# Pairs of tiles: softmax and z transfers in another place, sums of w_in in halves, a12 first in the closing pair

## The chip, the cores and the metric

One NeuronCore of a Trainium2 chip runs the program. The metric is the device time of one execution in microseconds; three runs of the kernel before gave 482.71, 483.19 and 483.50, and 483.19 is their median. Engines are named as in the profile: PE (TensorE), DVE (VectorE), ACT (ScalarE), POOL (GpSimd), SP (SyncE).

## The reference

Attention within chunks of 64 tokens (8 batches, 8 heads, 576 tokens, 64 wide), then a feed-forward layer with a SoLU and a layer norm on the 4608 x 512 result, all in float32:

```python
scores = scale * np.matmul(q_c, k_c.transpose(0, 1, 2, 4, 3))   # chunks of 64
attn = softmax(scores)                                          # with + 1e-09 in the sum
x = np.matmul(attn, v_c) -> (4608, 512)
h = x @ w_in                                                    # 512 -> 1024
solu = h * softmax(h)
ln = (solu - mean) / sqrt(var + 1e-06) * g_ln
return ln @ w_out                                               # 1024 -> 512
```

## The kernel before

**Tiles.** The 4608 tokens are 36 tiles of 128. Products in float32 are made of three fast ones: each operand is split into a rounded high part and a low rest (`x_top` and `x_bottom`, `z_top` and `z_bottom`, `wi_h` and `wi_l`), and high times low, high times high and low times high are summed in PSUM.

**Stages.** Tiles 0 to 4 run in an order written out by hand. Tiles 5 to 9 run singly in a loop (line 1212): `ffn_in` (24 matmuls), attention of two later tiles after each odd tile, and three thirds (`third`, 8 matmuls each) of the product with `w_out` of an earlier tile. Tiles 10 to 35 run in 13 pairs (`pair`, line 1108). A pair makes its h by Strassen's scheme, seven products of 6 matmuls each (`strassen`: a11, s2, s1, s3, then s4, a12, a22), in two PSUM banks pa and pb that alternate; between s3 and s4 and after the attention stand 24 matmuls each on `w_out` (`product`; PSUM tile po). The attention (`scores` and `values`, PSUM tiles sx and sy) of the tiles of the next pairs follows a22.

**Prepared sums.** Strassen's scheme wants sums of blocks of `w_in` (`t_sum`, `t_top`, `t_bottom` for t3 and t2; `t_quarter` for t1). POOL makes them while tiles 5 to 8 run: t3 in tile 5, t2 and two quarters of t1 in tile 6, the other two quarters in tile 8. The quarters go through a scratch tile of the name t_f. The tile `signs` (the identity and its negative, needed by `t_product` in the first pair) has the same tag t_f with one buffer, so it takes the scratch's place in memory.

**What sets the order.** From tile 5 on every engine works its instructions off in the order of the code. A wait of one instruction holds all that stand behind it on its engine. In a pair, `softmax_e` (ACT), `softmax_b` (a sum and a reciprocal on DVE, then a multiplication on POOL) and `attn_turn` (a transposition of 32 x 32 blocks on DVE into a_b, then 8 transfers of 64 KB into attn_t, 4 from SP and 4 from ACT or POOL) prepare the probabilities for the next `values`. `pair_moves` issues 16 transfers of 64 KB from z_b to z_t that bring the finished z of the pair before into its transposed place: 8 from SP at once, 8 from POOL through `issue`. `h_sum` is the DVE addition that empties pb, `act.copy(h0[:, left], a)` the copy on ACT that empties pa. The matmuls of s4, a12 and a22 carry the waits for all transfers that the attention reads (`waits`), one each. All recorded operations have the line of the recording helper, 50, in the profile.

Of the kernel before, what the change touches and what calls it, by code (L numbers as in the profile page):

```python
# [8 lines left out]
F32 = mybir.dt.float32  # L9
# [49 lines left out]
def chunk_attention_then_solu_ffn(  # L59
# [351 lines left out]
    def softmax_e(i):  # L411
        e = st[i, "e"]
        act.activation(e, e, AF.Exp, scale=SCALE)
# [387 lines left out]
    def whole(parts):  # L801
        for _ in parts:
            pass
# [56 lines left out]
    TW = {}  # L860
# [7 lines left out]
    def f32(w):  # L868
        return [x.bitcast(F32) for x in w]

    def t_sum(of, less, more=()):

        f = raw_t[0]
        if of is not None:
            pool.tensor_tensor(out=f, in0=f32(of)[0], in1=f32(of)[1], op=ALU.add)
        for x in f32(less):
            pool.tensor_tensor(out=f, in0=f, in1=x, op=ALU.subtract)
        for x in f32(more):
            pool.tensor_tensor(out=f, in0=f, in1=x, op=ALU.add)

    def t_room():
        def room(dt):
# [9 lines left out]
        return rest  # L892

    def t_top(name):
        pool.tensor_copy(out=TW[name][0], in_=raw_t[0])

    def t_bottom(name):
        high, low = TW[name]
        pool.tensor_tensor(out=low, in0=raw_t[0], in1=high.bitcast(F32), op=ALU.subtract)

    signs = []

# [45 lines left out]
    def x_top(i, n):  # L948
        f, (high, low) = XO[i][n]
        act.copy(high, f)  # L950

    def x_bottom(i, n):
        f, (high, low) = XO[i][n]
        pool.tensor_tensor(out=low, in0=f, in1=high.bitcast(F32), op=ALU.subtract)
# [25 lines left out]
    def h_sum(to, of, bank_):  # L980
        dve.tensor_tensor(out=to, in0=of, in1=bank_, op=ALU.add)
# [47 lines left out]
    def z_top(i, f=slice(0, NFC)):  # L1029
        zt, zh, _ = z_views(i)  # L1030
        act.copy(zh[:, f], zt[:, f])

    def z_bottom(i, f=slice(0, NFC)):
        zt, zh, zl = z_views(i)
        dve.tensor_tensor(
            out=zl[:, f], in0=zt[:, f], in1=zh[:, f].bitcast(F32), op=ALU.subtract
        )
# [65 lines left out]
    def issue(todo, n):  # L1103
        for f, args in todo[:n]:
            f(*args)
        del todo[:n]

    def pair(i):
        opening, closing = i == first_pair, i + 2 >= NT
        if not banks:  # L1110
            whole_h.close()
            ps_b = ctx.enter_context(tc.tile_pool(name="ps_b", bufs=1, space=PSUM))
            banks.extend(ps_b.tile([P, HALF], F32, name=n) for n in ("pa", "pb"))
        a, b = banks
        h0, h1 = (work.tile([P, FF], F32, name="z") for _ in range(2))
        HZ[i], HZ[i + 1] = h0, h1
        out1 = queue[0][0]
        softs = pending[:]
        pending.clear()
        zmoves = pair_moves(i - 2)  # L1120

        z_top(out1)
        strassen(i, "a11", a, B11)
        act.copy(h0[:, left], a)
        z_bottom(out1)
        for m in softs[:1]:
            softmax_e(m)
        strassen(i, "s2", b, TW["t2"])
        h_sum(h0[:, right], h0[:, left], b)
        x_top(i, "s3")  # L1130
        x_bottom(i, "s3")
        for m in softs[1:]:
            softmax_e(m)
        strassen(i, "s1", a, TW["t1"])
        issue(zmoves, 2)
        for m in softs:
            whole(softmax_b(m))
        evict()
        strassen(i, "s3", b, TW["t3"])
        if opening:  # L1140
            t_product("t4", B21, TW["t2"], 0)
        if not opening:
            spread(i - 1)
        for n in ("s4", "a12", "a22"):
            x_top(i, n)
        h_sum(h1[:, left], h0[:, right], b)
        x_bottom(i, "s4")
        for m in softs:
            attn_turn(m)
        issue(zmoves, 12)  # L1150
        least1 = h_out((h1[:, left], h1[:, right]), a, None)
        dve.tensor_tensor(out=h0[:, right], in0=h0[:, right], in1=a, op=ALU.add)
        for p in range(1 if closing else 3):
            product()
            if opening and p == 1:
                t_product("t4", B21, TW["t2"], 1)
        for n in ("a12", "a22"):
            x_bottom(i, n)
        if not opening:
            power(i - 2)  # L1160
            power(i - 1)
        for m in (i + 4, i + 5):
            if m < NT:
                turn(m)
        load_some(9)
        store_rest()

        out0 = queue[0][0]
        waits = (soon.pop(i + 2, []) + soon.pop(i + 3, []))[::-1]
        strassen(i, "s4", a, B22, waits, 6 * NCH2)  # L1170
        if not closing:
            kept.append(out1)
            evict()
            z_top(out0)
        least0 = h_out((h0[:, right], h0[:, right]), a, None)
        strassen(i, "a12", b, B21, waits, 3 * NCH2)
        least0 = h_out((h0[:, left], h0[:, left]), b, least0)
        strassen(i, "a22", a, TW["t4"], waits)
        pair_exp(i, 0, least0)
        least1 = h_out((h1[:, left], h1[:, left]), a, least1)  # L1180
        pair_exp(i, 1, least1)
        if closing:
            return
        z_bottom(out0)
        attention(i)
        for m in (i + 4, i + 5):
            if m < NT:
                load_v(m)
        x_pair(i + 2)
        x_sums(i + 2)  # L1190
        pair_mul(i)
        pair_mul(i + 1)
        for _ in range(3):
            product()
        kept.append(out0)
        pair_mean(i)
        spread(i)
        x_halves(i + 2)
        if i + 4 < NT:
            softmax_a(i + 4)  # L1200
            pending.append(i + 4)
        pair_mean(i + 1)
        pair_turn(i)
        if i + 5 < NT:
            softmax_a(i + 5)
            pending.append(i + 5)
        pair_turn(i + 1)
        load_some(9)
        store_rest()

    first_pair = PAIRS
    for i in range(first, first_pair):
        order.on = i >= ORD
        odd = i % 2 == 1
        turning = i + 1 == first_pair
        if i == first:
            z_turn(i - 1)
            load_batch(next_batch)
            next_batch += 1
        load_v(i + 3)  # L1220
        z_split(queue[0][0], slice(0, NFC))
        if not odd:
            softmax_e(i + 3)
            whole(softmax_b(i + 3))
            attn_turn(i + 3)
            x_high(i + 1)
            if i == first_pair - 4:
                t_sum(None, (), B11)
                t_top("t2")
                t_bottom("t2")  # L1230
                rest_of_room()
            if i == first_pair - 2:
                for x in range(2, 4):
                    t_quarter("t1", B12, B11, x)
        load_some(LOADS[i][0])
        whole(ffn_in(i))
        if odd:
            for m in (i + 1, i + 2):
                scores(m + 2)
                values(m)  # L1240
        if turning:
            load_v(i + 4)
        whole(solu_a(i))
        third()
        if i == first_pair - 5:
            rest_of_room = t_room()
            t_sum(B22, B12)
            t_top("t3")
            t_bottom("t3")
        if odd:  # L1250
            softmax_a(i + 3)
            softmax_e(i + 3)
            if turning:
                x_pair(i + 1)
                x_sums(i + 1)
            else:
                x_high(i + 1)
        else:
            x_low(i + 1)
        whole(solu_b(i))  # L1260
        if odd:
            if turning:
                x_halves(i + 1)
            else:
                x_low(i + 1)
            whole(softmax_b(i + 3))
            attn_turn(i + 3)
        else:
            for m in (i + 4, i + 5):
                turn(m)  # L1270
        third()
        variance(i)
        if i == first_pair - 4:
            for x in range(2):
                t_quarter("t1", B12, B11, x)
        third()
        load_some(LOADS[i][1])
        if turning:
            pair_turn(i)
            signs.append(work.tile([P, 2, P], F32R, name="signs", tag="t_f", bufs=1))  # L1280
            act.copy(signs[0][:, 0], ident)
            act.activation(signs[0][:, 1], ident, AF.Copy, scale=-1.0)
        else:
            z_turn(i)
        store_rest()
        if odd:
            softmax_a(i + 4)
            if turning:
                pending.append(i + 4)
# [55 lines left out]
```

## Time and profile before

| what | us |
|---|---|
| median of 3 runs | 483.19 |
| the profiled execution | 485.89 |
| its span, first to last instruction | 484.1 |
| PE busy | 462.5 (96%) |
| DVE busy | 373.4 (77%) |
| POOL busy | 312.8 (65%) |
| ACT busy | 287.2 (59%) |

PE is busy 96% of the span with 4123 matmuls, and the granted clock is 1.0 but for the first slices of the span (mean 0.995), which is the level of 2.4 GHz. A busy PE is what the records model, so a short wait may hide in it: it is better seen in the start times of matmuls that follow each other. The other engines matter where a matmul waits for them.

### The profile page before, as it was taken

Reading aid. Unit: us, or ns where it says so; the run is one execution under the profiler, and the core shown is the slowest. Engines: PE = TensorE matmul, PEld = TensorE weight load, DVE = VectorE, ACT = ScalarE, POOL = GpSimd, SP = SyncE. Lnnn points to the kernel's source line nnn. Section 1 sums busy time; section 2 is a strip of 40 time slices with the busy share of each in tenths; the row PEclk is TensorE's granted clock in tenths of the full one; section 3 lists DMA queues with packets and bytes.
Section 4 is the critical chain, followed back from the end, with each engine's and each line's share of the span. In section 5 each row is a group of like instructions: output and inputs, shape, how many; then the busy total and the mean of one; then the engine's idle time right before and its main releaser. Section 6 shows DMA issues by size and latency. Waiting matters only on the chain.

```text
span 484.1 us, 11452 instructions
## 1 busy us (share of the span) xinstructions
PE 462.5 (96%) x4123; PEld 361.8 (75%) x4123; DVE 373.4 (77%) x582; ACT 287.2 (59%) x511; POOL 312.8 (65%) x452
## 2 busy tenths in 40 slices
PE   6799999999998999999999989999999999999997
PEld 5655888777876777767777767787777777777776
DVE  2899987799876796969797969796979797955530
ACT  2675885446455393839393928383939393838451
POOL 0339458899986376766676766767667675758340
PEclk9899999999999999999999999999999999999999
DMA  9999888857795767776717866677681717141231
GB/s 231 297 235 320 140 142 175 178 143 157 150 188 123 153 134 161 161 157 140 199 27 163 156 157 149 155 166 169 148 197 32 193 35 184 43 135 49 61 108 43
DMA packets 193767, 72.06 MB, mean 149 GB/s; under 512 B 177128, under 2 KB 177648, under 8 KB 193328
## 3 DMA queue, kind: packets, MB, share of 16 engines
q1 hardware_dynamic: 186528, 58.63, 54.1%
q0 software_dynamic: 4736, 9.45, 8.0%
q10 hardware_dynamic: 2448, 3.28, 2.6%
q8 instruction: 32, 0.52, 0.5%
q14 instruction: 23, 0.19, 0.1%
HBM read 36.70 MB, written 9.44 MB: 95 GB/s over the span
## 4 chain that ended last, share of the span: by engine, by line
PE 56%; DMA 17%; SPq 9%; DVE 7%; ACT 5%; issue 3%; POOL 3%; ACTq 0%; DVEq 0%; POOLq 0%
PE po L50 26%; PE pa L50 10%; DMA attn_t<-a_b 10%; SPq L50 9%; PE ph L50 9%; DMA z_t<-z_b 5%; PE pb L50 5%; PE sx L50 4%; PE sy L50 3%; DMA nat_z<-in_q_dram 2%; ACT z_h L50 2%; DVE a_b L50 1%; ACT z L50 1%; DVE z_b L50 1%; DVE z L50 1%
## 5 line engine op out<-in xcount | busy, mean ns | idle before, releaser
L50 PE MATMUL po<-wo_l,z_h 128*128 128x512 f32 x280 | 111.2, 397 | 0.4 <-ACT z_h L50 0.4
L50 PE MATMUL po<-wo_h,z_l 128*128 128x512 f32 x280 | 109.7, 392 | 1.2 <-DVE z_l L50 1.2
L50 PE MATMUL po<-wo_h,z_h 128*128 128x512 f32 x280 | 109.5, 391 | 0.0
L50 POOL DMA_DIRECT2D z_t<-z_b x136 | 68.6, 510 | 10.9 <-DVE z_b L50 9.0
L50 POOL TENSOR_TENSOR x_s<-x_p 128x256 f32<-128x256 f32 x26 | 23.4, 899 | 68.2 <-ACT x_p L50 67.2
L50 POOL TENSOR_TENSOR x_t<-x_p,x_t 128x256 fp32r<-128x256 f32 x65 | 48.5, 757 | 24.8 <-ACT x_t L50 22.7
L50 PEld LDWEIGHTS po<-wo_h,z_l 128*128 128x128 f32 x280 | 52.6, 188 | 14.0 <-DVE z_l L50 3.0
L50 ACT ACTIVATE o_sb<-po,r 128x512 f32<-128x512 f32 (+1 forms) x36 | 24.4, 676 | 64.5 <-DMA attn_t<-a_b 46.3
L50 PEld LDWEIGHTS po<-wo_l,z_h 128*128 128x128 f32 x280 | 52.6, 188 | 12.3 <-ACT z_h L50 0.9
L50 PEld LDWEIGHTS po<-wo_h,z_h 128*128 128x128 f32 x280 | 52.6, 188 | 10.5
L50 DVE TENSOR_TENSOR z_l<-z_t,z_h 128x1024 fp32r<-128x1024 f32 (+1 forms) x36 | 43.6, 1210 | 12.8 <-ACT z_h L50 8.9
L50 ACT CAST z_h<-z_t 128x1024 fp32r<-128x1024 f32 (+1 forms) x36 | 34.9, 969 | 30.7 <-DMA attn_t<-a_b 17.1
L50 PE MATMUL pa<-wi_h,x_t 128*128 128x512 f32 x156 | 49.3, 396 | 2.2 <-DMA attn_t<-a_b 1.3
L50 DVE STREAM_TRANSPOSE z_b<-z 128x1024 f32<-128x1024 f32 x33 | 40.8, 1236 | 11.0 <-ACT z L50 5.8
L50 ACT ACTIVATE z<-z,z_sum 128x1024 f32<-128x1024 f32 x34 | 39.1, 1150 | 3.4 <-DVE z L50 3.2
L50 PE MATMUL pb<-t_w,x_t 128*128 128x512 f32 x156 | 40.8, 397 | 0.1
L50 POOL TENSOR_TENSOR e<-e,s_rinv 128x512 f32<-128x512 f32 x31 | 32.3, 1059 | 10.8 <-DVE s_rinv L50 10.4
L50 ACT ACTIVATE sq<-z 128x1024 bf16<-128x1024 f32 x36 | 37.6, 1046 | 2.5 <-POOL z L50 2.5
L50 PEld LDWEIGHTS pa<-wi_h,x_t 128*128 128x128 f32 x156 | 29.2, 188 | 11.2 <-DMA attn_t<-a_b 4.2
L50 ACT ACTIVATE z_b<-z,h_nmax 128x1024 f32<-128x1024 f32 x26 | 29.9, 1148 | 12.7 <-DVE h_nmax L50 12.2
L50 DVE SCALAR_TENSOR_TENSOR z<-z,z_b 128x1024 f32<-128x1024 f32 x26 | 36.2, 1426 | 0.0
L50 PEld LDWEIGHTS pb<-t_w,x_t 128*128 128x128 f32 x156 | 28.3, 188 | 10.4 <-ACT e L50 4.5
(140 smaller groups left out, 995.9 us busy)
## 6 DMA issues: line engine op xcount, KB each, us to landing
out_dram<-o_sb SPq DMA_DIRECT2D x35, 256.0 KB, 3.6
z_t<-z_b SPq DMA_DIRECT2D x128, 64.0 KB, 2.0
z_t<-z_b POOLq DMA_DIRECT2D x128, 64.0 KB, 2.6
q_st<-in_q_dram SPq DMA_DIRECT2D x96, 72.0 KB, 3.1
k_st<-in_k_dram SPq DMA_DIRECT2D x96, 72.0 KB, 2.9
v_sb<-in_v_dram SPq DMA_DIRECT2D x27, 256.0 KB, 5.0
w_raw<-in_moe_w_out_dram SPq DMA_DIRECT2D x4, 1024.0 KB, 9.3
attn_t<-a_b SPq DMA_DIRECT2D x60, 64.0 KB, 3.6
```

The source lines that it names most:

```text
L50: ins = make(*args, **kwargs)
```

## The change

Six edits, none of which changes what is computed:

- `t_sum`, `t_top` and `t_bottom` work on each of two halves of 512 columns in place of 1024 at once.
- In `pair`, the exponentials of the two softmax tiles move ahead (the first into the pair before, ahead of `x_halves`), then come the copy of a11's product, `x_top` of s3, `z_top`; `softmax_b` goes ahead of `h_sum`, `z_bottom` behind it.
- All 8 z transfers of POOL are issued together, behind the two multiplications of the softmax and ahead of the low part of s4.
- `attn_turn` moves ahead of the second `h_sum`.
- In the closing pair (tiles 34 and 35) the product a12 stands ahead of s4.
- `signs` is written at the end of tile 8 in place of the end of tile 9.

```diff
--- before.py
+++ after.py
@@ -870,13 +870,14 @@
 
     def t_sum(of, less, more=()):
 
-        f = raw_t[0]
-        if of is not None:
-            pool.tensor_tensor(out=f, in0=f32(of)[0], in1=f32(of)[1], op=ALU.add)
-        for x in f32(less):
-            pool.tensor_tensor(out=f, in0=f, in1=x, op=ALU.subtract)
-        for x in f32(more):
-            pool.tensor_tensor(out=f, in0=f, in1=x, op=ALU.add)
+        for m in range(NCH2):
+            f = raw_t[0][:, m]
+            if of is not None:
+                pool.tensor_tensor(out=f, in0=f32(of)[0][:, m], in1=f32(of)[1][:, m], op=ALU.add)
+            for x in f32(less):
+                pool.tensor_tensor(out=f, in0=f, in1=x[:, m], op=ALU.subtract)
+            for x in f32(more):
+                pool.tensor_tensor(out=f, in0=f, in1=x[:, m], op=ALU.add)
 
     def t_room():
         def room(dt):
@@ -892,11 +893,15 @@
         return rest
 
     def t_top(name):
-        pool.tensor_copy(out=TW[name][0], in_=raw_t[0])
+        for m in range(NCH2):
+            pool.tensor_copy(out=TW[name][0][:, m], in_=raw_t[0][:, m])
 
     def t_bottom(name):
         high, low = TW[name]
-        pool.tensor_tensor(out=low, in0=raw_t[0], in1=high.bitcast(F32), op=ALU.subtract)
+        for m in range(NCH2):
+            pool.tensor_tensor(
+                out=low[:, m], in0=raw_t[0][:, m], in1=high[:, m].bitcast(F32), op=ALU.subtract
+            )
 
     signs = []
 
@@ -1119,22 +1124,20 @@
         pending.clear()
         zmoves = pair_moves(i - 2)
 
-        z_top(out1)
+        for m in softs[-1:]:
+            softmax_e(m)
         strassen(i, "a11", a, B11)
         act.copy(h0[:, left], a)
-        z_bottom(out1)
-        for m in softs[:1]:
-            softmax_e(m)
+        x_top(i, "s3")
+        z_top(out1)
+        x_bottom(i, "s3")
+        for m in softs:
+            whole(softmax_b(m))
         strassen(i, "s2", b, TW["t2"])
         h_sum(h0[:, right], h0[:, left], b)
-        x_top(i, "s3")
-        x_bottom(i, "s3")
-        for m in softs[1:]:
-            softmax_e(m)
+        z_bottom(out1)
+        issue(zmoves, 8)
         strassen(i, "s1", a, TW["t1"])
-        issue(zmoves, 2)
-        for m in softs:
-            whole(softmax_b(m))
         evict()
         strassen(i, "s3", b, TW["t3"])
         if opening:
@@ -1143,11 +1146,10 @@
             spread(i - 1)
         for n in ("s4", "a12", "a22"):
             x_top(i, n)
+        for m in softs:
+            attn_turn(m)
         h_sum(h1[:, left], h0[:, right], b)
         x_bottom(i, "s4")
-        for m in softs:
-            attn_turn(m)
-        issue(zmoves, 12)
         least1 = h_out((h1[:, left], h1[:, right]), a, None)
         dve.tensor_tensor(out=h0[:, right], in0=h0[:, right], in1=a, op=ALU.add)
         for p in range(1 if closing else 3):
@@ -1167,14 +1169,18 @@
 
         out0 = queue[0][0]
         waits = (soon.pop(i + 2, []) + soon.pop(i + 3, []))[::-1]
+        if closing:
+            strassen(i, "a12", b, B21)
+            least0 = h_out((h0[:, left], h0[:, left]), b, None)
         strassen(i, "s4", a, B22, waits, 6 * NCH2)
         if not closing:
             kept.append(out1)
             evict()
             z_top(out0)
-        least0 = h_out((h0[:, right], h0[:, right]), a, None)
-        strassen(i, "a12", b, B21, waits, 3 * NCH2)
-        least0 = h_out((h0[:, left], h0[:, left]), b, least0)
+        least0 = h_out((h0[:, right], h0[:, right]), a, least0 if closing else None)
+        if not closing:
+            strassen(i, "a12", b, B21, waits, 3 * NCH2)
+            least0 = h_out((h0[:, left], h0[:, left]), b, least0)
         strassen(i, "a22", a, TW["t4"], waits)
         pair_exp(i, 0, least0)
         least1 = h_out((h1[:, left], h1[:, left]), a, least1)
@@ -1195,10 +1201,11 @@
         kept.append(out0)
         pair_mean(i)
         spread(i)
-        x_halves(i + 2)
         if i + 4 < NT:
             softmax_a(i + 4)
+            softmax_e(i + 4)
             pending.append(i + 4)
+        x_halves(i + 2)
         pair_mean(i + 1)
         pair_turn(i)
         if i + 5 < NT:
@@ -1277,12 +1284,13 @@
         load_some(LOADS[i][1])
         if turning:
             pair_turn(i)
+        else:
+            z_turn(i)
+        store_rest()
+        if i == first_pair - 2:
             signs.append(work.tile([P, 2, P], F32R, name="signs", tag="t_f", bufs=1))
             act.copy(signs[0][:, 0], ident)
             act.activation(signs[0][:, 1], ident, AF.Copy, scale=-1.0)
-        else:
-            z_turn(i)
-        store_rest()
         if odd:
             softmax_a(i + 4)
             if turning:
```

ACT at the end of tile 8 and of tile 9, around `signs` (x_t, x_p: operands of the first pair; o_sb: a finished output; z_h: high part of z; z, h_sum<-ph,h_nmax: the exponential of tile 9's h). Before, at the end of tile 9:

```order
L50 ACTIVATE sq,ssq<-z 128x1024
L50 ACTIVATE o_sb<-po,r 128x512
L50 CAST signs<-ident 128x128
L50 ACTIVATE signs<-ident 128x128
L50 CAST z_h<-z_t 128x1024
L50 COPY z<-pa 128x512
L50 ACTIVATE e_103<-e_103 128x4x128
```

Now, at the end of tile 8:

```order
L50 ACTIVATE sq,ssq<-z 128x1024
L50 ACTIVATE o_sb<-po,r 128x512
L50 CAST signs<-ident 128x128
L50 ACTIVATE signs<-ident 128x128
L50 CAST z_h<-z_t 128x1024
L50 ACTIVATE z,h_sum<-ph,h_nmax 128x1024
L50 ACTIVATE e_102<-e_102 128x4x128
```

The two writes of `signs` now stand ahead of tile 9's z_h and of all that ACT does for tile 9. In the built program the first of them waits for POOL, for the last subtraction of the last quarter of t1, which reads the scratch t_f; before, it had no wait.

DVE at the start of a pair (z_b: transposition of the last z of the pair before; s_sum, s_rinv: `softmax_b`; z<-z,pb: `h_sum`; z_l: `z_bottom`; a_b: `attn_turn`). Before:

```order
L50 STREAM_TRANSPOSE z_b<-z 128x8x4x32
L50 TENSOR_TENSOR z_l<-z_t,z_h 128x1024
L50 TENSOR_TENSOR z<-z,pb 128x512
L50 TENSOR_REDUCE s_sum<-e_102 128x8
L50 RECIPROCAL s_rinv<-s_sum 128x8
L50 TENSOR_REDUCE s_sum<-e_103 128x8
L50 RECIPROCAL s_rinv<-s_sum 128x8
L50 TENSOR_TENSOR z<-z,pb 128x512
L50 STREAM_TRANSPOSE a_b<-e_102 128x8x2x32
L50 STREAM_TRANSPOSE a_b<-e_103 128x8x2x32
```

Now:

```order
L50 STREAM_TRANSPOSE z_b<-z 128x8x4x32
L50 TENSOR_REDUCE s_sum<-e_102 128x8
L50 RECIPROCAL s_rinv<-s_sum 128x8
L50 TENSOR_REDUCE s_sum<-e_103 128x8
L50 RECIPROCAL s_rinv<-s_sum 128x8
L50 TENSOR_TENSOR z<-z,pb 128x512
L50 TENSOR_TENSOR z_l<-z_t,z_h 128x1024
L50 STREAM_TRANSPOSE a_b<-e_102 128x8x2x32
L50 STREAM_TRANSPOSE a_b<-e_103 128x8x2x32
L50 TENSOR_TENSOR z<-z,pb 128x512
```

Four instructions of the softmax stand ahead of the first addition out of pb, where z_l stood, and the transpositions a_b are ahead of the second.

POOL in a pair, from the softmax's multiplications (e) to the low parts of the last two products' operands (x_t). Before:

```order
L50 DMA z_t<-z_b 32x512 x2
L50 TENSOR_TENSOR e_102<-e_102,s_rinv 128x4x128
L50 TENSOR_TENSOR e_103<-e_103,s_rinv 128x4x128
L50 TENSOR_TENSOR x_t<-x_s,x_t 128x256
L50 DMA z_t<-z_b 32x512 x6
L50 TENSOR_TENSOR x_t<-x_p,x_t 128x256 x2
```

Now:

```order
L50 TENSOR_TENSOR e_102<-e_102,s_rinv 128x4x128
L50 TENSOR_TENSOR e_103<-e_103,s_rinv 128x4x128
L50 DMA z_t<-z_b 32x512 x8
L50 TENSOR_TENSOR x_t<-x_s,x_t 128x256
L50 TENSOR_TENSOR x_t<-x_p,x_t 128x256 x2
```

The multiplications no longer wait behind two transfers, the other six transfers are ahead of the low part of s4, and the closing pair has the same order without the multiplications.

## Rows read from the trace of the kernel before

**Rows 1.** Waits of PE, 160 to 440 us: in total, times, longest.

```profile
PE pa L50 <- DMA attn_t<-a_b: 2.6, 6, 0.7
```

**Rows 2.** Windows from attention to attention: length, busy by engine, PEclk, DMA share, GB/s.

```profile
408.85:431.94 23.09, 23.09 (x219) 18.57 (x218) 17.71 (x29) 13.74 (x27) 16.35 (x25) 1.00 0.41 112
sum 264.35, PE 259.91 PEld 203.40 DVE 218.27 ACT 165.11 POOL 181.07; mean PE 23.63 PEld 18.49 DVE 19.84 ACT 15.01 POOL 16.46
```

**Rows 3.** Timeline of PE in one pair: start, length, operation, tiles, [idle before].

```profile
346.85 1.52 PE L50 MATMUL pb<-t_w,x_t 128*128 128x512 f32 x6
...
349.86 1.62 PE L50 MATMUL pb<-t_w,x_t 128*128 128x512 f32 x6
```

**Rows 4.** Waits of PE from 425 us to the end, as in rows 1.

```profile
PE po L50 <- DVE z_l L50: 0.5, 1, 0.5
PE pa L50 <- DVE z L50: 0.4, 1, 0.4
PE pa L50 <- ACT z L50: 0.4, 1, 0.4
PE po L50 <- ACT z_h L50: 0.4, 2, 0.2
```

**Rows 5.** Groups of POOL by form, 84 to 142: busy, mean ns, idle before.

```profile
L50 POOL TENSOR_TENSOR t_w<-t_w,wi_l 128x1024 f32<-128x1024 f32 x2 | 4.8, 2419 | 0.2
```

**Rows 6.** Timeline of DVE at 88 us.

```profile
88.69 3.34 DVE L50 TENSOR_TENSOR z_l<-z_t,z_h 128x1024 fp32r<-128x1024 f32 x1 [0.86 <-ACT z_h L50]
```

**Rows 7.** Timeline of POOL, last quarter of t1, 136 to 142 us.

```profile
138.05 1.60 POOL L50 TENSOR_TENSOR t_f<-t_f,wi_h 128x256 f32<-128x256 f32 x1
...
141.01 0.73 POOL L50 TENSOR_TENSOR t_w<-t_f,t_w 128x256 fp32r<-128x256 f32 x1
```

**Rows 8.** Timeline of ACT, end of tile 8 and of tile 9.

```profile
136.19 1.05 ACT L50 CAST z_h<-z_t 128x1024 fp32r<-128x1024 f32 x1 [0.62 <-DMA attn_t<-a_b]
...
150.07 0.29 ACT L50 CAST signs<-ident 128x128 fp32r<-128x128 f32 x1
...
151.41 0.58 ACT L50 COPY z<-pa 128x512 f32<-128x512 f32 x1
151.89 0.63 ACT L50 ACTIVATE e<-e 128x512 f32<-128x512 f32 x1
```

**Rows 9.** Timeline of DVE in tile 9.

```profile
140.32 1.23 DVE L50 TENSOR_REDUCE h_nmax<-ph 128x1 f32<-128x1024 f32 x1 [1.26 <-PE ph L50]
```

**Rows 10.** Timeline of PE in the first pair.

```profile
152.04 1.67 PE L50 MATMUL pa<-t_w,x_t 128*128 128x512 f32 x6 [1.31 <-ACT z L50]
...
164.21 0.70 PE L50 MATMUL pa<-wi_h,x_t 128*128 128x512 f32 x2 [0.91 <-DVE kT L50]
```

**Rows 11.** Timeline of DVE at the start of a pair.

```profile
347.93 1.18 DVE L50 TENSOR_TENSOR z_l<-z_t,z_h 128x1024 fp32r<-128x1024 f32 x1
349.03 0.68 DVE L50 TENSOR_TENSOR z<-z,pb 128x512 f32<-128x512 f32 x1
349.63 0.68 DVE L50 TENSOR_REDUCE s_sum<-e 128x8 f32<-128x520 f32 x1
...
350.47 0.64 DVE L50 TENSOR_REDUCE s_sum<-e 128x8 f32<-128x520 f32 x1
...
352.19 1.48 DVE L50 STREAM_TRANSPOSE a_b<-e 128x512 f32<-128x512 f32 x2
```

**Rows 12.** Timeline of ACT at the same place.

```profile
344.96 0.41 ACT L50 CAST x_t<-x_p 128x256 fp32r<-128x256 f32 x1 [1.05 <-POOL x_p L50]
```

**Rows 13.** Timeline of POOL in the same pair.

```profile
350.87 2.06 POOL L50 TENSOR_TENSOR e<-e,s_rinv 128x512 f32<-128x512 f32 x2
...
353.56 2.97 POOL L50 DMA_DIRECT2D z_t<-z_b  x6
```

**Rows 14.** Windows of the same pair, as in rows 2.

```profile
353.00:355.00 2.00, 2.00 (x11) 1.65 (x10) 2.00 (x5) 0.00 (x0) 2.00 (x4) 1.00 0.40 98
355.00:360.00 5.00, 5.00 (x22) 3.70 (x20) 3.38 (x9) 0.69 (x1) 4.39 (x10) 1.00 0.92 227
```

## The prediction

> **What bounds the kernel now.** I read the windows first, then the waits of PE, then timelines of the places that the diff touches. In the window behind the last attention of the pairs PE is busy for all of its 23.09 us at a granted clock of 1.00, and the eleven windows before and with it, one for each attention of the pairs, sum to 264.35, of which PE is busy 259.91 [rows 2]. So PE sets the time: an edit gains only what it takes from the waits of PE, and it loses what it adds to them. In the pairs most of these waits are for the attention's transfers: 2.6 us in six waits of the bank pa [rows 1], and some more of pb. A busy row of matmuls can hide a little waiting: eleven windows of 23.09 would be 253.99, so up to 10.4 us of the eleven depend on neighbours. Much of that is work of POOL, DVE and ACT that some pairs must wait for; only the waits for attn_t, with the refill behind each (5 us by my reading, half of it in rows 1), are touched by the diff. The rest of PE's waits stands at the end: four of 0.4 to 0.5 us behind 425 us [rows 4].
>
> The sum is made on the profiled execution, 485.89 us, whose span is 484.1. It is 0.6% above the median 483.19; I apply the differences to the median, as the waits are of the same length in both by a first estimate.
>
> **Sums of w_in in halves, with `signs` ahead.** POOL's two-input operations take 2.419 us on 1024 columns [rows 5] and 0.73 on 256 [rows 7]; the line through both gives 1.30 on 512, so an operation split in two costs 2 x 1.30 - 2.42 = 0.18, and 0.26 with one more start of 0.08 between (the gap between POOL's rows in tile 8). Five operations of t3 and four of t2 are split: 9 x 0.26 = 2.3 us on POOL. The bound below zero: the softmax's multiplications, also 512 wide with two inputs, step by about 1.05 (two in 2.06) [rows 13], by which a split would save 0.24, or 9 times about 1.5 to 2 us. I take 1.30, as the sums read operands of the form that the line was made from.
>
> Who waits for POOL there? In before nobody on PE, as the quarters of t1 end at 141.01 + 0.73 = 141.74 [rows 7] and t1 is first read later. Now the first write of `signs` waits for that last subtraction, and it stands in ACT's queue ahead of tile 9's z_h, which in before ran from 136.19 for 1.05 [rows 8]. One thing comes back: POOL's row at 138.05 took 1.60 where its like takes 0.73 [rows 7], as DVE's two-input z_l ran beside it; z_l now comes after it, so 0.85 is saved. The last quarter ends at 141.74 + 2.3 - 0.85 = 143.2 (139.4 to 144). Behind it come the two writes (about 0.46 in all with the wait's end), z_h 1.05, z_l 1.1, and only then DVE's h_nmax of tile 9: 143.2 + 2.64 = 145.85, where it started at 140.32 [rows 9]: 5.5 us later. Tile 9's exponential, its x_p copies and the chain over POOL to the first operands of the first pair stand in line behind that. They have no slack to swallow it: at the first pair PE already waited 1.31 for ACT's copy of pa [rows 10], which started at 151.41 [rows 8]. Back come 0.82, as between 150.07 and that copy stood two writes and z_h (1.34) and now one exponential (its row is 0.63, about 0.5 of it to the next start) [rows 8], and 0.67 of the 0.91 that PE waited for the attention's k at 164.21 [rows 10], since a_b moves up by one h_sum in the first pair too. 5.5 - 0.8 - 0.7 = **+4.1**, from +0.2 (POOL 1.5 sooner, 139.4) to +4.8.
>
> In tile 5, where t3 is made, z_l took 3.34 [rows 6], blocked by POOL's 1024-column row; with halves about 1 us of that goes. But the transfers that POOL issues behind the sums go out later by about 1.7 and PE meets them at the next attention: 0, from -0.9 to +1.5.
>
> What the row of 3.34 shows is that a z_l beside a two-input operation of POOL waits for the end of it. The Trainium skill says the same ("SBUF — State Buffer", section "Who interferes with whom"): DVE and GpSimd share a port pair as an exclusive lock, a DVE operation with two SBUF inputs contends with GpSimd's reads, and the second blocks wholly. It speaks for halves (a shorter lock) and against the next part, where z_l is put right behind POOL's multiplications: by it a_b gains the 0.3 of the next part, without it 1.0, and the pairs' sum would be nearer to its lower end of -4.0.
>
> **The pair, eleven windows.** Before, DVE does z_l (347.93) and then h_sum (349.03) [rows 11]; s2 ends at 346.85 + 1.52 = 348.37, and s3, which needs the bank that h_sum empties, starts at 349.86 [rows 3], 0.15 after h_sum's end. So s3 already hangs on h_sum. Now two pairs of sum and reciprocal stand in z_l's place. From one to the next is 350.47 - 349.63 = 0.84 [rows 11], so h_sum starts at 347.93 + 1.68 = 349.61, **0.58 later** than before, in each pair. That is a new wait of PE; s1 cannot cover it, as it has run by then. The exponential that moves into the pair before costs nothing: ACT waited 1.05 for x_p where it will stand [rows 12], against 0.63 for the exponential [rows 8]; were that cover gone, x_t would come 0.63 later.
>
> For this the waits for attn_t go. `attn_turn` moves ahead of the second h_sum, POOL's multiplications no longer stand behind two transfers and s1's stretch, and POOL's z transfers, six of which issue from 353.56 [rows 13], are out by then. In before the 16 DMA engines stand at a share of 0.40 from 353 to 355 and at 0.92 from 355 to 360 [rows 14]: the z transfers move out of the full stretch into the empty one, and the attention's have it to themselves. The a_b themselves, at 352.19 [rows 11], come only about 0.3 earlier, as z_l now stands ahead of them and is blocked by POOL's multiplications (without the block it would be 1.0). A window then is 23.09 + 0.58 = 23.67, and eleven are 260.4; I add 0.7 for waits that stay: 261.1 - 264.35 = **-3.3**, from -1.4 (all 2.6 of rows 1 stay) to -4.0 (none stays).
>
> **Behind the last attention.** PE waits at 433 and 434 for z_h (0.2) and z_l (0.5) [rows 4], with 0.27 of refill at each; the last z transfers of POOL land before the attention's, so both go: **-1.25** (-1.3 to 0).
>
> **The closing pair.** With a12 ahead of s4 the waits for ACT's z (0.4), DVE's z (0.4) and one z_h (0.2) [rows 4], with refill 1.6 in all, go, since between a product and the reader of its bank lies another product. But a12's low operand is made by POOL, behind all eight z transfers (six take 2.97, so eight about 4.0 [rows 13]) and the low part of s4, which a12 did not have to wait for: I put this new wait at 0.95. Sum **-0.65**, from -1.6 to +0.3.
>
> **Rivals.**
> - *The pairs gain more or POOL loses less.* If halves go as the multiplications do (1.05), the quarters end at 139.4 and the start costs 0.2 rather than 4.1: 478.2; if only part of this holds, about 480. For it: the multiplications are the nearest rows in width. Against: they are fed by a broadcast reciprocal, another form of operand.
> - *The transfers land no sooner.* If the engines are the limit and not the place of issue, 2.6 us of waits stay and the pairs give -1.4: 484.0. For it: share 0.92 [rows 14]; against it: 0.40 just before. The Trainium skill's rule ("DMA: Bandwidth & Descriptors", section "Issuing engines are not separate DMA queues") is that all transfers run on the same 16 engines whoever starts them; the stretch of 0.92 agrees, the dip before it does not bear on it.
> - *Slower: the wait of `signs` at its full size.* If POOL gets no 0.85 back, the last quarter ends at 144, the start costs 4.8, and if the waits for attn_t stay in part (-1.6) and the closing pair's new wait eats its gain (0), the sum is +4.8 - 1.6 - 1.25 = +2.0: 485.1. It decides as soon as the start costs more than the 5.2 that the other three parts give.
>
> **How the numbers follow.** 483.19 + 4.1 - 3.3 - 1.25 - 0.65 = **482.1** (chance 0.40). About 480: 0.22. 484.0: 0.20. 485.1: 0.18. Range 479.5 to 484.9: below, half of the first term's span (2.6 less); above, just under the slower rival. About 0.2%, 1.0 us, is what a measurement of this kernel can tell: faster than 482.2, slower than 484.2. The forecast lies at that edge, so a little over half of it and all of the 480 case count as faster (0.46), the rest of it and most of the 484.0 case as the same (0.29), the slower rival and a part of the 484.0 case as slower (0.25).
>
> **What the profile after would show.** Right: sums of 512 columns at 1.30 on POOL; ACT idle from about 136 to 143 ahead of the cast to signs, and h_nmax of tile 9 near 146, with waits of PE of about 4 us between 142 and 165; s3 of each pair waiting for DVE's h_sum, 0.58 later than now; no waits for attn_t; windows near 23.67; none for z_h and z_l at the last attention; in the closing pair one wait of a12 for POOL's x_t. Wrong: windows above 24 with waits for attn_t, sums near 1.05, or an ACT that passes `signs` with no idle time.

## The result: slower, and the profile after

The changed kernel takes 487.93 us (median of 4) where the kernel before took 483.05 beside it: a ratio of 1.0104 (95% interval 1.0082 to 1.0127), 4.9 us slower. The forecast was 482.1, and the range ended at 484.9. The profiled execution after spans 486.5 us.

The shown execution of before (span 484.1) is one of its slower ones, so before was profiled once more (the run b_again below, span 482.5), and that trace is the better measure. Here both are cut at the starts of the attentions. The rows give length, busy time of PE, PEld, DVE, ACT and POOL with instructions, the granted clock, DMA share and GB/s. First before, in its second profile:

```profile
89.23:115.22 25.99, 24.79 (x226) 19.89 (x225) 24.45 (x29) 12.54 (x21) 25.24 (x24) 1.00 0.78 159
115.22:140.98 25.76, 24.78 (x225) 19.75 (x224) 20.80 (x31) 12.64 (x20) 24.09 (x35) 1.00 0.85 172
140.98:168.34 27.36, 25.17 (x227) 19.97 (x226) 19.03 (x31) 13.71 (x27) 16.43 (x27) 1.00 0.64 134
168.34:430.81 262.47, 258.56 (x2400) 204.09 (x2399) 218.25 (x363) 165.25 (x308) 180.90 (x275) 1.00 0.64 142
430.81:482.50 51.69, 46.62 (x283) 37.48 (x282) 22.13 (x35) 27.73 (x50) 19.85 (x36) 1.00 0.20 62
```

And the same stretches after:

```profile
89.18:119.04 29.86, 26.68 (x225) 20.74 (x224) 22.89 (x29) 12.64 (x21) 28.53 (x32) 0.94 0.86 159
119.04:143.06 24.02, 24.02 (x226) 19.91 (x225) 19.23 (x29) 11.48 (x19) 21.68 (x35) 1.00 0.76 161
143.06:174.11 31.05, 26.11 (x228) 19.80 (x227) 21.01 (x32) 14.79 (x28) 16.98 (x28) 1.00 0.57 118
174.11:434.13 260.02, 252.42 (x2400) 205.00 (x2399) 224.47 (x363) 168.97 (x309) 181.30 (x275) 1.00 0.62 143
434.13:486.50 52.37, 46.37 (x283) 37.56 (x282) 22.76 (x35) 26.74 (x49) 20.42 (x35) 1.00 0.19 61
```

Row by row: +3.9 in tiles 5 to 7, where t3 is made; -1.7 in tiles 7 to 9; +3.7 from there through the first pair, where `signs` waits; -2.5 in the eleven windows of the pairs; +0.7 behind the last attention. The waits of PE after, in total, times and longest, over the whole span, name the places:

```profile
PE pb L50 <- DVE z L50: 7.6, 11, 0.9
PE ph L50 <- DMA attn_t<-a_b: 2.9, 2, 2.6
PE po L50 <- ACT z_h L50: 2.2, 2, 2.0
...
PE pa L50 <- DVE h_nmax L50: 0.9, 1, 0.9
...
PE pb L50 <- POOL x_t L50: 0.6, 1, 0.6
```

The first line is s3 waiting for h_sum in eleven pairs; it stands where [rows 1] had the attention's transfers, which no longer appear for pa. The second is tile 7, the third `signs` (2.0 of it), the last two are the closing pair.

The split between the first two rows depends on the execution: in the runs with the sums whole (pool_late aside) the first stretch takes 26.0 to 27.5 us and the second 24.5 to 25.9. Their sum, 50.8 to 51.8 there but for one run (pairs_closing, 53.3), is 53.9 after, so that 2 to 3 us stay of the +3.9, and 2.2 against b_again.

### The profile page after: what moved, and what is told of

Same layout as the page of the kernel before. It is cut to its first block, busy times and chain, and to the rows that moved or that the text cites. A ratio compares the mean times of both kernels' runs of the same rounds, so it can differ in the third digit from the quotient of the medians.

```text
span 486.5 us, 11435 instructions
## 1 busy us (share of the span) xinstructions
PE 456.0 (94%) x4123; PEld 364.3 (75%) x4123; DVE 379.0 (78%) x582; ACT 289.9 (60%) x511; POOL 315.1 (65%) x461
## 3 DMA queue, kind: packets, MB, share of 16 engines
q10 hardware_dynamic: 2448, 3.28, 2.3%
## 4 chain that ended last, share of the span: by engine, by line
PE 48%; DVE 17%; POOL 13%; ACT 8%; DMA 6%; issue 4%; SPq 2%; DVEq 0%; ACTq 0%; POOLq 0%
PE po L50 21%; PE pa L50 8%; PE pb L50 7%; PE ph L50 6%; POOL x_p L50 5%; PE sx L50 3%; DVE z_b L50 3%; DVE s_sum L50 3%; ACT z L50 3%; DVE z L50 3%; PE sy L50 3%; POOL x_t L50 2%; DMA nat_z<-in_q_dram 2%; POOL x_s L50 2%; SPq L50 2%
## 5 line engine op out<-in xcount | busy, mean ns | idle before, releaser
L50 ACT ACTIVATE o_sb<-po,r 128x512 f32<-128x512 f32 (+1 forms) x36 | 24.5, 681 | 68.9 <-DMA attn_t<-a_b 43.6
L50 DVE TENSOR_TENSOR z_l<-z_t,z_h 128x1024 fp32r<-128x1024 f32 (+1 forms) x36 | 50.9, 1413 | 16.8 <-ACT z_h L50 12.2
```

The source lines that it names most:

```text
L50: ins = make(*args, **kwargs)
```

## The experiments

All times are medians, the ratios are to the kernel before on the same chip. The medians of that kernel beside the runs lie between 483.05 and 484.27, so a difference between times of different groups of runs is good to about 1 us; where it matters, the traces are compared stretch by stretch.

**b_again**: before, unchanged.

> The kernel before, unchanged, profiled once more. The shown profile of before lasted 485.89 us where the timed runs have a median of 483.05, so 2.8 us of waits in it may be of that execution alone. Theory 'its waits for attn_t vary': the new profile is near 483 and PE waits for attn_t between 160 and 440 us are under 2 us, where they were 3.6 (2.6 of pa and 1.0 of pb). Rival 'profiling adds it everywhere': about 486 again with the same waits.

483.92 us, ratio 0.9998 (0.9979 to 1.0018); single runs lie between 481.9 and 485.6. The profiled span was 482.5, and the eleven windows sum to 262.47, where [rows 2] had 264.35. So the theory holds in its direction: 1.9 us of the windows in [rows 2] were of that execution. The waits did not vanish, though: 3.1 us for attn_t in ten places, where under 2 was expected.

**pairs_alone**: before with the edits inside the pairs alone (the hunks on `softmax_e`, `softmax_b`, `z_bottom`, `issue`, `attn_turn`).

> Before with the edits inside the pairs only (exponentials, softmax_b, z_bottom, z transfers, attn_turn), without the halves, without signs ahead, without a12 first. Theory 'each edit has its own place': the trace of after gains 4.4 us on before from 165 to 433 us, so 478.7; if the waits for attn_t of the shown profile were partly of that execution (see b_again), the gain is 4.4 - 2.4 = 2 and the time 481. Rival 'the pairs are where the loss is' (the new wait of s3, 0.62 in eleven pairs, is not paid back in timed runs): 483.05 + 2 or more, 485.

478.85 us, ratio 0.9896 (0.9867 to 0.9925): 5.2 faster. The pairs are not where the loss is. The sum of its windows is 259.85, as after. Against b_again its trace is 2.6 shorter in the windows, 1.05 in the stretch with the first pair (26.31 for 27.36) and 0.7 behind the last attention; a further 1.4 lies ahead of 88 us, in code that the edits do not touch. There the granted clock was 0.50 from 19.0 to 25.8 us in b_again, and 1.00 all the time there in pairs_alone.

**signs_back**: after with `signs` at its old place.

```diff
         if turning:
             pair_turn(i)
-        else:
-            z_turn(i)
-        store_rest()
-        if i == first_pair - 2:
             signs.append(work.tile([P, 2, P], F32R, name="signs", tag="t_f", bufs=1))
...
+        else:
+            z_turn(i)
+        store_rest()
```

> After with signs written at the end of tile 9 again, all else as in after. Theory: the offset between the traces of before and after grows from 3.0 to 6.5 us between 142 and 171 us, all of it the wait of signs, so 487.9 - 3.5 = 484.4. Rival 'POOL is late anyway': the quarters of t1 come so late that the first pair waits for them or for x_t without signs too: 487 or more.

484.14 us, ratio 1.0002 (0.9985 to 1.0018), 3.8 less than after. PE's wait of 2.0 for z_h is gone, the waits for attn_t in tile 7 (3.0) are not. The theory holds.

**whole_sums**: after with the three functions on 1024 columns again (first two hunks undone).

> After with the sums of w_in made whole (1024 columns) again, signs still ahead. Theory: the waits of ph for attn_t near 115 us (2.9 in all, with 3.5 of offset) come from the halves, which hold POOL's transfers back; without them 3.5 less there, and signs' wait ends about 2 us sooner for POOL but the same z_h chain stands behind: 487.9 - 3.5 = 484.4, to 483 if signs gains too. Rival 'those waits are a matter of when DMA engines are busy, not of the halves': no change, 487.5 or more.

484.08 us, ratio 1.0001 (0.9984 to 1.0017), 3.85 less than after. Between 80 and 172 us no wait for attn_t of note is left, while the wait of `signs` stands: on ACT (start, length, operation, idle time before and what ended it)

```profile
141.38 0.30 ACT L50 CAST signs<-ident 128x128 fp32r<-128x128 f32 x1 [5.77 <-POOL t_w L50]
```

**halves_t2**: after with halves for t2 alone.

```diff
-        for m in range(NCH2):
+        for m in range(NCH2) if of is None else (slice(0, NCH2),):
```

(the same condition, by the name of the sum, stands in `t_top` and `t_bottom`)

> After with halves for t2 (made in tile 6) only; t3 (made in tile 5) whole again. Theory 't3's halves hold back the transfers of z and attn that POOL issues behind them': the waits for attn_t near 115 us go as in whole_sums, so 487.9 - 3.5 = 484.4; the rest of the halves, t2's, only delays the quarters by about 1 us ahead of signs, 0 to 1 more than whole_sums (484.1). Rival 't2's halves, beside those transfers, are what costs': 487 or more.

484.87 us, ratio 1.0013 (0.9992 to 1.0035). Most of the halves' cost is in t3's: 3.1 of 3.85 go with them. What t2's cost, 0.8 by the medians, is not clear of the 1 us between groups.

**pool_late**: pairs_alone, sums whole, with t3's low part taken twice, so that POOL is busy longer at that place.

```diff
             t_bottom("t3")
+            t_bottom("t3")
```

> As pairs_alone (478.85; sums whole), but the low part of t3 is taken twice, so that POOL is busy 2.4 to 3.3 us longer in tile 5 without any halves. Theory 'the halves hurt by making POOL late: the transfers of z and attn that it issues behind the sums land later': waits for attn_t of 2 to 3 us near 113 us, 481 to 482. Rival 'it is the form of the halves (more, shorter locks of the port beside DVE) that hurts': no such wait, 479.

483.87 us, ratio 0.9988 (0.9972 to 1.0004): 5 slower than pairs_alone, more than expected: by the traces 2.9 of it lie in the stretch with t3 (29.41 for 26.54) and 0.7 in the next. Four waits for attn_t (2.1) appear, and one for DVE's z_l, which comes while POOL makes the low part again:

```profile
105.04 0.50 PE L50 MATMUL po<-wo_h,z_l 128*128 128x512 f32 x1 [1.06 <-DVE z_l L50]
...
114.73 0.50 PE L50 MATMUL ph<-wi_h,x_h 128*128 128x512 f32 x1 [0.44 <-DMA attn_t<-a_b]
116.77 0.50 PE L50 MATMUL ph<-wi_h,x_h 128*128 128x512 f32 x1 [0.72 <-DMA attn_t<-a_b]
```

So a late POOL is enough for the waits of tile 7; no halves are needed. Two of the four, 1.2 us, stand in the stretch with t3; as much again (1.1) is z_l's, behind the added operation.

**pairs_closing**: before with the edits in the pairs and a12 first in the closing pair.

> Before with the edits in the pairs and a12 first in the closing pair; sums whole and signs at its old place. In the trace of after PE has two new waits in the closing pair (POOL x_t 0.55, DVE h_nmax 0.94) for two that go. Theory 'closing costs about 1': 478.85 + 1.0 = 479.9. Rival 'as predicted, it gains': 478.2. And the sum of parts: signs_back (484.14) has the halves beside this, whole_sums (484.08) has signs beside this, so if the edits add up, halves and signs cost 4.2 each here, and after (487.9) is this plus 8.

481.13 us, ratio 0.9936 (0.9902 to 0.9970). The intervals of this and pairs_alone overlap, so the traces decide: matmul by matmul this one lies 1.4 us behind pairs_alone ahead of the closing pair and 2.7 at its end, so a12 first costs 1.35. In pairs_alone PE waits once in this place, 0.44 for DVE's z; here, on PE:

```profile
443.51 0.74 PE L50 MATMUL pb<-wi_h,x_t 128*128 128x512 f32 x2 [0.56 <-POOL x_t L50]
...
446.59 0.47 PE L50 MATMUL pa<-wi_l,x_t 128*128 128x512 f32 x1 [0.94 <-DVE h_nmax L50]
```

The end of every trace says the same: from the last attention of the pairs it takes 51.0 to 51.1 us in the runs with s4 first and the pairs' edits, and 52.3 to 52.4 in those with a12 first. Here pairs_alone, pairs_closing and the next run, closing_bank:

```profile
425.58:476.60 51.02, 46.09 (x283) 37.65 (x282) 22.79 (x35) 26.84 (x49) 20.43 (x35) 1.00 0.20 63
426.98:479.30 52.32, 46.37 (x283) 37.55 (x282) 22.78 (x35) 26.72 (x49) 20.42 (x35) 1.00 0.20 61
427.55:478.70 51.15, 46.12 (x283) 37.64 (x282) 22.79 (x35) 26.71 (x49) 20.42 (x35) 0.99 0.20 63
```

With signs_back (484.14) this run gives the halves' price, 3.0; with whole_sums (484.08) that of `signs`, 2.95. 481.13 + 3.0 + 2.95 = 487.1, of the 487.93 of after.

**closing_bank**: pairs_closing with a22 of the closing pair in the other bank.

```diff
-        strassen(i, "a22", a, TW["t4"], waits)
+        last = b if closing else a
+        strassen(i, "a22", last, TW["t4"], waits)
```

> As pairs_closing (481.13; closing pair with waits of 0.56 for POOL x_t and 0.94 for DVE h_nmax), but in the closing pair a22 goes to bank pb, which a12 left one product before, in place of pa, which s4 has just filled. Theory 'a12 first puts s4 and a22 on one bank back to back': the wait for h_nmax goes with its refill, 1.1 less, 480.0, and the step from 441 to 448 us is 1.1 shorter than in pairs_closing. Rival 'DVE is late in the chain and is waited for later': the wait moves to the thirds behind it, no change, 481.

479.19 us, ratio 0.9880 (0.9841 to 0.9919). The step as such is seen in the trace: a22 starts behind s4 without a wait, and matmul by matmul this trace goes from 0.6 us behind pairs_closing's to 0.6 ahead of it there.

```profile
446.05 0.40 PE L50 MATMUL pb<-wi_l,x_t 128*128 128x512 f32 x1
```

The end takes 51.15, about what it takes in pairs_alone: with the other bank a12 first costs nothing, and gains nothing.

**z_late**: pairs_alone with six of POOL's z transfers behind the low part of s4.

```diff
-        issue(zmoves, 8)
+        issue(zmoves, 2)
...
         x_bottom(i, "s4")
+        issue(zmoves, 6)
```

> As pairs_alone (478.85), but only two of POOL's z transfers go before the low part of s4 and six behind it, near their old place. It takes the early z transfers out of the edits in the pairs. Theory of the prediction 'the z transfers leave the full stretch and the attention's gain by it': without it waits for attn_t come back, 0.2 to 0.4 a pair, 481 to 483. Rival 'the earlier softmax and attn_turn do it alone' (all transfers share the 16 engines, whoever issues them and when): no waits for attn_t, 478 to 479.5.

479.91 us, ratio 0.9886 (0.9848 to 0.9925), the same as pairs_alone within the intervals; and no wait for attn_t came back. So the place of these six transfers has no part in the gain of the pairs that this can measure. What is left of the edits there is the earlier softmax and `attn_turn`, with z_l behind h_sum; no run takes these apart.

**sum_between** and **sum_first**: pairs_alone with h_sum between the two softmax sums, or ahead of both.

```diff
-        for m in softs:
+        for m in softs[:1]:
             whole(softmax_b(m))
         strassen(i, "s2", b, TW["t2"])
         h_sum(h0[:, right], h0[:, left], b)
+        for m in softs[1:]:
+            whole(softmax_b(m))
```

> As pairs_alone (478.85), but h_sum of s2 stands between the two softmax sums on DVE instead of behind both: 0.84 us earlier. Theory 's3 waits 0.62 in eleven pairs for nothing but h_sum's place in DVE's queue': s3's waits go, 478.85 - 6.8 = 472.0. Rival 'the attention's transfers then become the wait': the second tile's multiplication, its transposition and 8 transfers come about 0.5 later while PE comes 0.6 earlier, the waits for attn_t come back and 476 or more remains.

> As pairs_alone, but h_sum ahead of both softmax sums. s3's wait goes as in sum_between; DVE idles about 0.4 for s2 behind z_b and the whole softmax comes 1.1 later. Theory of sum_between without slack in the transfers: 472 here too. Rival: waits for attn_t return more strongly than there, 476 to 479.

sum_between 479.64 us, ratio 0.9909 (0.9880 to 0.9939); sum_first 487.71, ratio 1.0077 (1.0052 to 1.0102). s3's wait is gone in both, and others stand in its place. Waits of PE from 160 to 440 us in sum_between:

```profile
PE pa L50 <- DMA attn_t<-a_b: 3.5, 9, 0.8
```

and in sum_first:

```profile
PE po L50 <- DVE z_l L50: 8.6, 12, 0.7
PE pa L50 <- DMA attn_t<-a_b: 4.1, 8, 1.3
```

Neither kernel came near the 472 of the theory. In sum_between the rival was right. In sum_first it named only a part: the time lies far above its 476 to 479, and most of the waits are for z_l, which neither side had named. Where h_sum goes ahead, what stands behind it is late next.

**between_z_late**: sum_between, with POOL's z transfers late as in z_late.

> As sum_between (479.64, attn_t waits of 0.2 to 0.75 in nine pairs and no wait of s3), with POOL's z transfers late as in z_late, so that fewer transfers run beside the attention's. Theory 'the attention's transfers there wait for their share of the engines': attn_t waits shrink by half or more, 476. Rival 'they wait for the multiplication and the transposition of the second tile, not for engines': same waits, 479 to 480.

478.61 us, ratio 0.9879 (0.9844 to 0.9914). The waits for attn_t shrink from 3.5 to 1.6, in two places, which speaks for a share of the engines that the z transfers take there (one trace of each; in the two traces of before the same waits were 3.6 and 3.1). In their place come waits for z_l (1.6 in three places from 160 to 440 us, for 0.7 in sum_between). The theory had the waits right, but not its 476: the time is that of pairs_alone within its interval.

pairs_alone is the smallest version that beats both: 0.9896 of before, 9 us less than after. closing_bank, z_late and between_z_late (0.9879 to 0.9886) cannot be told from it.

## Why the prediction was wrong, step by step

**The base.** The prediction took its differences from an execution of 485.89 us and applied them to a median of 483.19, "as the waits are of the same length in both". They were not: the windows were 264.35 there and 262.47 in b_again. The pairs were forecast at 261.1; they came out at 260.02, 1.1 better than that. But 1.9 of the forecast gain of 3.3 had been of that one execution, so the gain against b_again is 2.5.

**t3 in tile 5: the step that failed most.** It stood at 0, from -0.9 to +1.5, and it is +3.9, of which 1.7 come back by the next attention. The size of the halves was right in sum, though not by parts: t3 is made on POOL in 14.0 us (89.24 to 103.22) in place of 12.1 (88.59 to 100.66), t2 in 9.7 (111.26 to 120.92) for 9.3 (107.58 to 116.91), together 2.2 for the forecast 2.3, where five splits for t3 and four for t2 had been put at 1.3 and 1.0. A row takes 1.26 to 1.30 where nothing blocks it. DVE did get its z_l back (no wait near 92 us). What failed is the 0, by which PE loses no more to the late transfers than it wins on z_l. On POOL in b_again:

```profile
102.29 4.02 POOL L50 DMA_DIRECT2D z_t<-z_b  x8
106.30 1.96 POOL L50 DMA_DIRECT2D attn_t<-a_b  x4
```

and after:

```profile
90.60 2.16 POOL L50 TENSOR_TENSOR t_w<-t_w,wi_h 128x512 f32<-128x512 f32 x1
...
104.61 4.02 POOL L50 DMA_DIRECT2D z_t<-z_b  x8
108.62 0.50 POOL L50 DMA_DIRECT2D attn_t<-a_b  x1
109.47 0.50 POOL L50 DMA_DIRECT2D attn_t<-a_b  x1 [0.35 <-DMA z_t<-z_b]
110.26 0.98 POOL L50 DMA_DIRECT2D attn_t<-a_b  x2 [0.29 <-issue]
```

The stretch starts at the same time in both (89.23 and 89.18). So the attention's first transfer from POOL is issued 2.3 later, where 1.7 was expected. It is also longer under way. Its time from issue to landing, in b_again and after:

```profile
DMA to landing us min/median/max: 3.3/3.3/3.3
DMA to landing us min/median/max: 5.4/5.4/5.4
```

It lands 4.4 later, at 114.0 for 109.6. The DMA share is 1.11 from 108 to 111 us and 1.38 from 111 to 114 after, and 0.90 to 0.97 from 106 to 110 in b_again, which speaks for busier engines; no run tests that. In b_again the matmul that carries the wait for this transfer runs at 112.57, 2.9 behind the landing, and waits for nothing. After, PE is ready for it 1.0 earlier, at 111.5 (114.10 - 2.56), as its waits for z_l and z ahead of it are 0.9 shorter: 4.4 - 2.9 + 1.0 = 2.5 is the wait. The matmul in b_again:

```profile
112.57 0.39 PE L50 MATMUL ph<-wi_h,x_h 128*128 128x512 f32 x1
```

and after, with the one that waits for POOL's third transfer:

```profile
114.10 0.50 PE L50 MATMUL ph<-wi_h,x_h 128*128 128x512 f32 x1 [2.56 <-DMA attn_t<-a_b]
...
115.76 0.80 PE L50 MATMUL ph<-wi_h,x_h 128*128 128x512 f32 x1 [0.31 <-DMA attn_t<-a_b]
```

So there was slack, but less than the delay, and the time that PE won on DVE's z_l went into the wait. The prediction read neither the slack nor the landing from a row. (The wait of 0.3 at 113.58 in the first profile of before was for a transfer that SP issues, not for one of POOL's.)

The 2.16 in the first of POOL's rows after is the block again, in both directions: DVE's z_l took 2.26 (from 89.34) as it came behind POOL's first half, and POOL's next half, 1.29 alone, waited for z_l. In b_again POOL's second row waits in the same way (3.25 at 91.73, where its like takes 2.42). The Trainium skill's rule ("SBUF — State Buffer", section "Who interferes with whom"), that of two such operations the second blocks wholly, agrees; shorter halves shorten DVE's wait (2.26 for 3.34 in [rows 6]) but not POOL's (0.87 for 0.83).

whole_sums and halves_t2 show that the lateness of after is t3's halves', and pool_late that a late POOL is enough for such waits. Of the 1.7 us that come back by the next attention (second row of the windows) 1.0 lie where b_again waited for v_sb (0.8) and attn_t (0.2) near 138 us and after for nothing.

**`signs`: right, in mechanism and about in size.** Forecast +4.1 from tile 9 through the first pair (its own terms, 5.53 - 0.82 - 0.67, give 4.0), measured 31.05 - 27.36 = +3.7. The chain is the forecast one:

```profile
145.56 0.30 ACT L50 CAST signs<-ident 128x128 fp32r<-128x128 f32 x1 [6.56 <-POOL t_w L50]
...
146.10 1.04 ACT L50 CAST z_h<-z_t 128x1024 fp32r<-128x1024 f32 x1
```

The last quarter ends at 145.53 and DVE's h_nmax starts at 148.32, 2.79 behind it (forecast 2.64). Against [rows 9] that is 8.0 later, of which 2.85 had been lost by the attention at 143.06: 5.15 for the forecast 5.5. The +3.7 is a net figure, as the forecast was: the pairs' edits take 0.7 to 1.05 from this stretch. The same stretch in pairs_alone (sums whole, `signs` at its old place), whole_sums (`signs` ahead) and signs_back (halves, `signs` at its old place):

```profile
139.42:165.73 26.31, 25.09 (x227) 20.12 (x226) 19.86 (x31) 13.61 (x27) 16.10 (x27) 1.00 0.70 141
140.82:169.93 29.11, 26.12 (x228) 19.81 (x227) 21.00 (x32) 14.78 (x28) 15.24 (x25) 1.00 0.62 128
143.22:169.86 26.64, 25.05 (x228) 20.12 (x227) 19.50 (x31) 13.61 (x27) 17.86 (x29) 1.00 0.68 139
```

So the wait of `signs` costs 2.8 with the sums whole (2.95 by the medians of whole_sums and pairs_closing) and 4.4 with the halves, which make POOL's last quarter later still.

**The pairs: the new wait as forecast, the reason for the gain not.** h_sum was to come 0.58 later; s3 now waits

```profile
352.35 0.93 PE L50 MATMUL pb<-t_w,x_t 128*128 128x512 f32 x3 [0.62 <-DVE z L50]
```

and the window is 260.02 / 11 = 23.64, for the forecast 23.67 and a bit. Nothing of the waits for attn_t stays. That the sum came out is in part luck: the prediction says that the diff touches only some 5 us of the 10.4 that the windows lose to their neighbours, yet by starting from eleven windows of 23.09 it takes nearly all of them away. The windows side with the sum: PE has 7.6 of new waits for h_sum over the eleven pairs, and still they are 2.5 shorter than in b_again, so some 10 us of losses are gone. Only 3.1 of these stood in b_again as waits for attn_t; most of the rest was hidden in rows that count as busy (PE 258.56 there, 252.42 after). But the part of the argument about the z transfers, that they leave the full stretch for the empty one, is not borne out by z_late: with six of the eight back near the old place the time is the same and no wait returns. The block of z_l by POOL's multiplications is there too (1.93 at 352.13 on DVE, forecast as a danger), without harm.

**Behind the last attention: failed.** -1.25 was forecast. z_h's wait is gone, but in b_again it wasn't there to begin with, and z_l's, 0.4 there, is 0.7 after: DVE starts z_l only behind the h_nmax of a22

```profile
434.91 0.08 DVE L50 DVE_READ_ACCUMULATOR2_ANT h_nmax<- 128x1 f32 x1
435.38 1.22 DVE L50 TENSOR_TENSOR z_l<-z_t,z_h 128x1024 fp32r<-128x1024 f32 x1 [0.39 <-issue]
```

1.6 us after z_h was done (432.69 + 1.05). So it hangs on a22 and on its place in DVE's queue, not on the transfers. It stood behind that h_nmax before too (in b_again z_l starts at 431.72, right behind it), so earlier transfers could not take its wait away; what the last 0.39 is, the records don't show. What the pairs' edits did bring behind the last attention is 0.7 (51.02 in pairs_alone for 51.69 in b_again), from another wait: PE no longer waits 0.4 for ACT's z in the closing pair, a gain that the prediction had put down to a12 first.

**The closing pair: wrong sign.** -0.65 was forecast, from -1.6 to +0.3; it is +1.35 in pairs_closing. The wait for POOL's x_t was foreseen, at 0.95 (it is 0.56). DVE's z no longer appears, ACT's z had gone with the pairs' edits, and the z_h of 0.2 stays. What failed is the sentence that "between a product and the reader of its bank lies another product". With a12 ahead, s4 and a22 use pa back to back, and PE waits 0.94 for DVE to empty it. closing_bank, which gives a22 the other bank, takes that wait away.

**The sum.** The spans of after and b_again differ by +4.0, for -1.1 forecast. Of these 5.1, tiles 5 to 9 make 2.2 (+3.9 and -1.7 for 0), the base of the pairs 0.8 (-2.5 for -3.3), the end 2.6 (+0.7 for -1.9; 2.0 of it in the closing pair), and `signs` -0.4 (+3.7 for +4.1). The slower rival named `signs`, and its place was right; but `signs` doesn't outweigh the rest by itself. Two terms turned the sign: t3, where the prediction had put nothing, and the closing pair, where it had put a gain. With these two as forecast the same sum would give -0.2. By whole_sums the halves cost 3.85 in all, about as much as `signs` by signs_back (3.8): 2.2 in tiles 5 to 9, and 1.9 in that they make the wait of `signs` longer (31.05 for 29.11).

## What to carry to other kernels

Before work is added to an engine, list what it issues behind that work, and read from the trace how much slack each of these has between its landing and its reader (here 2.9 us, for a delay of 4.4). A reader that comes earlier by another part of the change has less. When products change their order, write down the bank of each and look for two neighbours on one bank. And take the base from more than one profiled execution where the metric's single runs spread by as much as the terms of the sum.

## What the runs showed of the hardware

A long wait of PE cost more than itself in one place. Behind the wait of 2.56 us, and about the 0.31 that follows it, the granted clock fell to its lower level of 1.2 GHz (0.50) and stayed there to 119 us (length, busy times, clock, DMA share, GB/s):

```profile
114.00:115.00 1.00, 0.90 (x4) 0.54 (x4) 1.00 (x2) 0.48 (x1) 1.00 (x1) 1.00 1.40 142
115.00:116.00 1.00, 0.69 (x3) 0.38 (x3) 1.00 (x1) 0.00 (x0) 0.92 (x2) 0.81 1.02 108
116.00:117.00 1.00, 1.00 (x3) 0.81 (x4) 0.20 (x1) 0.00 (x0) 1.00 (x1) 0.50 0.68 105
117.00:118.00 1.00, 1.00 (x3) 0.77 (x3) 0.00 (x0) 0.00 (x0) 1.00 (x3) 0.50 0.89 137
118.00:119.00 1.00, 1.00 (x3) 0.33 (x1) 0.00 (x0) 0.00 (x0) 1.00 (x2) 0.50 1.13 291
```

In pool_late the clock stays at 1.00 here, behind waits of 0.44 and 0.72. From the matmul behind the second wait to the start of the attention (sx), 3.28 us pass after (115.76 to 119.04) and 1.87 in pool_late (116.77 to 118.64):

```profile
118.64 0.69 PE L50 MATMUL sx<-kT,qT 64*64 64x64 f32 x32
```

So about 1.4 of the 3.9 in tiles 5 to 7 is the clock's. signs_back shows the same fall behind the same wait (2.6); the wait of 2.05 us for z_h at 147 us was followed by no fall.
